# Fused attention, memory and expert kernel: scores of two heads as one step, padded memory tiles, one pace for attention

## The chip, the cores and the metric

The kernel runs on one core of one Trainium2 chip. The metric is the device time of one execution in microseconds (us). Before the change the median of three runs is 653.46 us (652.81 to 653.50).

## What is computed

The reference does two things in a row. The first is attention with a compressive memory, for 4 batches, 8 heads, 576 tokens and a head width of 64:

```
scores = q @ k.T / 8, causal
local  = softmax(scores) @ v
q_p    = elu(q) + 1
mem    = (q_p @ M_prev) / (q_p @ z_prev + 1e-6)
x      = g * mem + (1 - g) * local          # g = sigmoid(beta), one number per head
```

The second is a gated expert over all 2304 tokens, where `x` now has 512 columns (8 heads of 64):

```
out = (sigmoid(x @ w_gate) * (x @ w_val)) @ w_out      # 512 -> 1536 -> 512
```

Every product must keep single precision. The kernel gets there in two ways: as a plain fp32 matmul, which TensorE records as two instructions, or as three cheaper fp32r products of a high part and a remainder (high by high, high by low, low by high).

## The kernel before

**Groups.** The 2304 tokens are cut into six groups of 384 rows. Group 0 and group 5 hold the last 192 rows of two batches each ("tail" groups); groups 1 to 4 hold the first 384 rows of one batch each. Per group there is an attention part with four pairs of heads, and an expert part (`moe`) with 12 blocks of 128 hidden columns. The expert part of a group needs the attention results `xh`, `xl` of that group (high part and remainder, transposed).

**Attention of a pair.** The two heads of a pair lie on partitions 0 to 63 and 64 to 127 of a tile `kp`, so that the score matmul of one head uses the upper half of TensorE's rows and that of the other head the lower half. `scores` runs three times for a pair, one for each block of 128 queries. Up to the ninth pair (`n < SPLIT`) the scores are plain fp32 matmuls from `kp`; from then on they are fp32r products from split keys `kq`. Each head has a PSUM bank of its own. VectorE (DVE) adds the mask and finds the row's extreme in one pass (L505), ScalarE (ACT) takes the exponential (L514), `turn` transposes the result (on TensorE for pairs 0 to 7 and the last, by DMA in between), `values` multiplies by `v`, and `across` transposes the pair's `x` and writes `xh` on ACT and `xl` on DVE. `memory` multiplies the feature map `ph` by the tile `mb`, which holds `M_prev` and `z_prev` of two heads in block-diagonal form. GpSimd fills `mb` with zeros once (L298), and two DMAs of 66 KB write the two blocks.

**Expert.** For each block `f`: 24 matmuls of 384 columns (gate and value), then a tanh, a product, a copy and a subtraction that alternate between ACT and DVE, and nine matmuls of 512 columns of the block before (`down`). In group 0 the weights come as float64 and are converted on ACT and DVE first (`convert`: three tiles per block, four DVE instructions of 512 columns for each: L665, L667, L670 and a subtraction at L251); the result goes to DRAM, and groups 1 to 5 load it from there.

**What sets the order.** Nothing is issued while the Python loops run. Each instruction is recorded as a step with an engine, an estimated cost, the keys that it reads and writes, and a place in line (`Program.add`). `Program.issue` then plays all steps through a list schedule: whenever an engine is free, it takes the ready step that is first in line. The order of the instructions on each engine is what this yields, and the engines follow it strictly. Steps of TensorE in attention are moved up in line by 150 places (`LEAD`), and the estimated cost of TensorE is doubled up to `COLD`. The place in line comes from the main loop: while the expert part of group g is recorded, the ten steps per pair of group g + 1 are recorded between its pieces, spread by `SPREAD`.

Of the kernel before, what the change touches and what calls it, by code (L numbers as in the profile page):

```python
# [8 lines left out]
F32 = mybir.dt.float32  # L9
# [11 lines left out]
SPLIT = 9  # L21
# [4 lines left out]

SPREAD = 0.94


WHEN = (20, 36)  # L30

COLD = 12.0

# [11 lines left out]
class Program:  # L45
# [58 lines left out]
    def issue(self):  # L104
# [7 lines left out]
        engines = sorted({o[0] for o in ops})  # L112
        free = dict.fromkeys(engines, 0.0)
        link = 0.0
# [5 lines left out]
        for _ in ops:  # L120
# [16 lines left out]
            if e == "pe" and at < COLD:  # L137
                cost *= 2
            free[e] = at + cost
# [14 lines left out]
def tile_attention_memory_moe(  # L154
# [9 lines left out]
    nc = tc.nc  # L164
# [131 lines left out]

    def zeros(t, k):
        pool(520, lambda: nc.gpsimd.memset(t.rearrange("p b c -> p (b c)"), 0.0), [],  # L298
             [k + (j,) for j in range(2)], fast=True)

    def half(t, k):
# [14 lines left out]
    xl_r = Ring("xl", [128, KD, GT], F32R, 2)  # L316
    mb_r = Ring("mb", [128, HP, 2 * MC], F32, 2, init=zeros)
    ph_r = Ring("ph", [128, GT], F32, 2)
# [46 lines left out]
    def load_unit(g):  # L365
        mem[g] = []
        for b in batches(g):
            m, mk = mb_r.take()
            for j in range(2):
                r = slice(64 * j, 64 * j + 64)  # L370
                load(m[r, :, MC * j:MC * j + MC], mz[b, r].rearrange("p (a c) -> p a c", a=HP), 66, [], [mk + (j,)])
            mem[g].append((m, [mk + (j,) for j in range(2)]))

# [76 lines left out]
    def split(n):  # L450
# [8 lines left out]
        for e, (kp, kk) in enumerate(u.kp):  # L459
            for j in range(2):  # L460
# [8 lines left out]
                u.kq[j].append((kq, [kh, kd, kl], q, [kx, ql[j][1] + ("z",)]))  # L469

    def scores(n, c):

# [7 lines left out]
        def part(i, k0, k1):  # L480
# [8 lines left out]
            with pg.block():  # L489
                for e, q, m0, m1 in es * (n < SPLIT):  # L490
                    kp, kk = u.kp[e]
                    for j, r in enumerate(js):
                        pe(2 * m / 2385.0 + (0.07 if pair else 0.21), lambda kp=kp, j=j, r=r, q=q, m0=m0, m1=m1: nc.tensor.matmul(  # L493
                            out=sp[j][0][m0:m1, :m], lhsT=kp[r, u.qa + q:u.qa + q + m1 - m0],
                            rhs=kp[r, u.ka + k0:u.ka + k1], start=True, stop=True), [kk], [sp[j][1]])
                for e, q, m1 in ([(1, 64, 128), (0, 128, 64)] if pair else [(es[0][0], q0, 128)]) * (n >= SPLIT):
                    for j in range(2):
                        kq, kk, ql, kx = u.kq[j][e]
                        keys = kq[:, u.ka + k0:u.ka + k1]
                        out, out_k = sp[j][0][:m1, :m], sp[j][1]  # L500
                        matmul(out, kq[:, u.qa + q:u.qa + q + m1], keys, m, kk, [out_k], True, False)
                        matmul(out, ql[:, q:q + m1], keys, m, kk + kx, [out_k], False, True)
# [287 lines left out]

    def count(g):

        return HP * 10

    constants()
# [11 lines left out]
    att_banks[:] = [5, 6, 7]  # L807
    ready = 0
    for g in range(NG):
        while ready < g:  # L810
            y = step()
            if y:
                ready = y[1]
        done = 0
        steps = count(g) if g + 1 < NG else 0
        for i, _ in enumerate(moe(g)):
            while done * (7 * NF + 1) * SPREAD < (i + 1) * steps and ready == g:
                done += 1
                y = step()
# [10 lines left out]
def _layout(q, k, v, M_prev, z_prev, beta, moe_w_gate, moe_w_val, moe_w_out):  # L830
# [9 lines left out]
    mz = np.concatenate([M_prev, z_prev[..., None]], axis=3)  # L840
    mz = mz.reshape(B, H // 2, 2, D, D + 1).transpose(0, 2, 3, 1, 4)

    def up(x):
# [5 lines left out]
        "vp": vz,  # L849
        "mz": mz.reshape(B, 2 * D, (H // 2) * (D + 1)),  # L850
        "beta": beta,
# [25 lines left out]
```

## Time and profile before

| | |
|---|---|
| median of the runs | 653.46 us |
| the profiled execution | 652.48 us |
| its span, first to last instruction | 650.7 us |
| TensorE (PE) busy | 637.8 us, 98% |
| weight load (PEld) busy | 560.0 us, 86% |
| VectorE (DVE) busy | 422.0 us, 65% |
| ScalarE (ACT) busy | 303.5 us, 47% |
| GpSimd (POOL) busy | 8.6 us, 1% |
| DMA | 136.34 MB, mean 210 GB/s |

"Busy" is the time in which an engine has at least one instruction in flight. Matmuls overlap, so the mean duration of one (342 ns for 384 columns) is longer than the step from one to the next. The share of busy time is a mean over the whole span; the stages differ. Up to about 59 us only attention runs, from 59 us to about 172 us attention and the first expert part with the conversion of weights, then attention and expert parts without conversion, and from 574 us the last expert part alone.

### The profile page before, as it was taken

The numbers are of one execution on the slowest core, as the hardware profiler recorded it, in microseconds if no ns is written. First come the engines' busy times: TensorE is split into PE (matmuls) and PEld (weight loads), VectorE is DVE, ScalarE is ACT, GpSimd is POOL, SyncE is SP. The second block draws the span as 40 slices with busy tenths as digits, with TensorE's granted clock in tenths as the row PEclk, the third lists the DMA queues.
The fourth block names the chain that finished last, engine by engine and source line by source line (L and its number), as shares of the span: only waits on it lengthen the run. The fifth ranks groups of instructions, "written<-read, shape, count | busy, mean of one in ns | idle before, by whom it ended". The sixth has DMA issues, their size and how long they took to land.

```text
span 650.7 us, 12265 instructions
## 1 busy us (share of the span) xinstructions
PE 637.8 (98%) x4776; PEld 560.0 (86%) x4776; DVE 422.0 (65%) x1142; ACT 303.5 (47%) x590; POOL 8.6 (1%) x52
## 2 busy tenths in 40 slices
PE   6999999999999999999999999999999999999996
PEld 3656887878899999999999999989898899999995
DVE  3899989899837667656775656766757684411112
ACT  5878675667634424524543633433625242421111
POOL 3000000000000000000000000000000000000000
PEclk9999999999999999999999999999999999999999
DMA  8457878787996777779768879868879765264452
GB/s 291 159 195 225 285 261 304 233 320 240 245 295 197 180 201 209 218 207 223 202 178 214 219 204 201 210 177 249 252 181 219 174 183 157 74 235 145 179 171 72
DMA packets 90121, 136.34 MB, mean 210 GB/s; under 512 B 65744, under 2 KB 67792, under 8 KB 80848
## 3 DMA queue, kind: packets, MB, share of 16 engines
q1 hardware_dynamic: 90064, 135.57, 72.2%
q8 instruction: 37, 0.61, 0.4%
q14 instruction: 20, 0.16, 0.1%
HBM read 104.09 MB, written 17.30 MB: 187 GB/s over the span
## 4 chain that ended last, share of the span: by engine, by line
PE 92%; DVE 4%; DMA 2%; issue 1%; POOL 0%; ACT 0%; SPq 0%; POOLq 0%; DVEq 0%; ACTq 0%
PE bank L228 73%; PE bank L232 10%; PE bank L493 5%; PE bank L235 4%; DMA tl_wr<-pl_wr 1%; DMA mb<-in_mz_dram 1%; DVE a L505 1%; DVE kq_wt L251 0%; DVE ql L251 0%; DVE wt L667 0%; DVE wt L670 0%; DVE at L536 0%; DVE xm L251 0%; DVE xs L251 0%; DVE gl L251 0%
## 5 line engine op out<-in xcount | busy, mean ns | idle before, releaser
L228 PE MATMUL bank<-xh,wg 128*128 128x384 f32 x576 | 166.2, 342 | 0.2
L228 PE MATMUL bank<-xh,sv 128*128 128x384 f32 x576 | 165.5, 341 | 0.0
L228 PE MATMUL bank<-sv,gh 128*128 128x512 f32 x432 | 141.9, 399 | 0.0
L751 DVE SCALAR_TENSOR_TENSOR th<-th,bank 128x384 f32<-128x384 f32 x72 | 39.7, 551 | 116.4 <-PE bank L228 111.8
L228 PEld LDWEIGHTS bank<-xh,wg 128*128 128x128 f32 x576 | 105.0, 188 | 7.8 <-issue 3.0
L228 PEld LDWEIGHTS bank<-xh,sv 128*128 128x128 f32 x576 | 105.1, 188 | 1.4 <-issue 0.7
L514 ACT ACTIVATE a<-a,st 128x512 f32<-128x512 f32 (+4 forms) x144 | 81.5, 583 | 35.9 <-DVE st L505 35.3
L228 PE MATMUL bank<-xl,wg 128*128 128x384 f32 x288 | 97.7, 339 | 0.0
L228 PE MATMUL bank<-xl,sv 128*128 128x384 f32 x288 | 97.4, 338 | 0.0
L228 PEld LDWEIGHTS bank<-sv,gh 128*128 128x128 f32 x432 | 79.2, 188 | 12.5 <-issue 1.2
L749 ACT ACTIVATE th<-bank 128x384 f32<-128x384 f32 x72 | 35.2, 489 | 117.1 <-PE bank L228 116.7
L228 PE MATMUL bank<-sv,gl 128*128 128x512 f32 x216 | 85.9, 398 | 0.0
L241 ACT CAST gh<-th 128x384 fp32r<-128x384 f32 x72 | 36.8, 511 | 94.8 <-DVE th L751 94.3
L505 DVE CUSTOM_DVE_ANT_0 a<-bank,mask 128x128 f32<-128x128 f32 (+4 forms) x144 | 68.3, 485 | 19.0 <-PE bank L493 10.2
L228 PEld LDWEIGHTS bank<-xl,wg 128*128 128x128 f32 x288 | 54.1, 188 | 3.3 <-issue 0.5
L536 DVE COPY at<-tl_wr 128x256 uint16<-128x256 uint16 (+3 forms) x90 | 46.5, 519 | 15.5 <-DMA tl_wr<-pl_wr 15.3
L228 PEld LDWEIGHTS bank<-xl,sv 128*128 128x128 f32 x288 | 54.1, 188 | 0.6 <-issue 0.3
L251 DVE TENSOR_TENSOR gl<-th,gh 128x384 fp32r<-128x384 f32 x72 | 40.0, 555 | 20.4 <-ACT gh L241 19.9
L241 ACT CAST kq_wt<-kp 64x768 fp32r<-64x768 f32 (+2 forms) x60 | 38.0, 637 | 21.4 <-PE bank L228 20.5
L228 PEld LDWEIGHTS bank<-sv,gl 128*128 128x128 f32 x216 | 40.6, 188 | 8.3 <-issue 0.5
L493 PE MATMUL bank<-kp 64*128 64x512 f32 (+5 forms) x156 | 38.9, 523 | 4.0 <-DMA kp<-in_qk_dram 4.0
L530 DVE COPY pl_wr<-a 128x256 uint16<-128x256 uint16 (+3 forms) x90 | 41.7, 468 | 0.2
(72 smaller groups left out, 729.2 us busy)
## 6 DMA issues: line engine op xcount, KB each, us to landing
sv<-w SPq DMA_DIRECT2D x60, 1024.0 KB, 5.4
wr<-in_w_dram SPq DMA_DIRECT2D x36, 512.0 KB, 4.4
kp<-in_qk_dram SPq DMA_DIRECT2D x32, 384.0 KB, 3.8
w<-sv SPq DMA_DIRECT2D x12, 1024.0 KB, 6.4
out_dram<-ob SPq DMA_DIRECT2D x14, 256.0 KB, 5.0
vt<-in_vp_dram SPq DMA_DIRECT2D x8, 330.0 KB, 4.7
vr<-in_vp_dram SPq DMA_DIRECT2D x8, 330.0 KB, 5.4
vt<-in_vp_dram SPq DMA_DIRECT2D x8, 198.0 KB, 4.3
```

The costliest lines, as they stand in the source:

```text
L228: lambda: nc.tensor.matmul(out=out, lhsT=lhsT, rhs=rhs, start=start, stop=stop), r, w)
L232: lambda: nc.tensor.matmul(out=out, lhsT=lhsT, rhs=rhs, start=start, stop=stop), r, w)
L235: pe(0.110, lambda: nc.tensor.transpose(out=out, in_=in_, identity=identity), r, w)
L241: act(n, lambda: nc.scalar.copy(out=out, in_=in_), r, w)
L251: dve(n, lambda: nc.vector.tensor_tensor(out=out, in0=in0, in1=in1, op=op), r, w)
L493: pe(2 * m / 2385.0 + (0.07 if pair else 0.21), lambda kp=kp, j=j, r=r, q=q, m0=m0, m1=m1: nc.tensor.matmul(out=sp[j][0][m0:m1, :m], lhsT= ...
L505: dve(m + 60, lambda aj=aj, sj=sj, pj=pj: nc.vector.tensor_tensor_reduce(out=aj[:, k0:k1], in0=pj[:, :m], in1=mk, scale=-0.125, scalar=3.0 ...
L514: act(W + 120, lambda aj=aj, sj=sj: nc.scalar.activation(out=aj[:, :W], in_=aj[:, :W], func=AF.Exp, scale=-1.0, bias=sj[:, len(ns) - 1:len ...
L530: dve(2 * W, lambda src=src, pl=pl: nc.vector.tensor_copy(out=pl.rearrange("p (two w) -> p two w", two=2), in_=src), [ak], [pk], fast=True)
L536: dve(2 * W, lambda tl=tl, dst=dst: nc.vector.tensor_copy(out=dst, in_=tl.rearrange("p (two w) -> p two w", two=2)), [lk], [key], fast=True)
L749: act(GT, lambda: nc.scalar.activation(out=th, in_=pg_[:, :GT], func=AF.Tanh, scale=0.5), [pg_k], [th_k])
L751: dve(GT, lambda: nc.vector.scalar_tensor_tensor(out=th, in0=th, scalar=1.0, in1=pv[:, :GT], op0=ALU.add, op1=ALU.mult,), [th_k, pv_k], [t ...
```

## The change

The two heads' score matmuls of a piece become one step of the schedule, so nothing can be placed between them, and the step waits for both heads' banks. `mb` is laid out with its zeros by the host and comes in one DMA of 266 KB; the fill on GpSimd is gone. The steps of attention are no longer counted anew in each group: one count runs through all groups, ten steps per pair, with a lead of `AHEAD` = 8. The planner's constants are other ones: the higher cost of TensorE at the start is 1.5 times up to 8 us (2 times up to 12 us before), and all engines start at 0.7.

```diff
-SPREAD = 0.94
+AHEAD = 8
...
-COLD = 12.0
+COLD = 8.0
+
+START = 0.7
...
-        free = dict.fromkeys(engines, 0.0)
+        free = dict.fromkeys(engines, START)
...
             if e == "pe" and at < COLD:
-                cost *= 2
+                cost *= 1.5
...
-    mb_r = Ring("mb", [128, HP, 2 * MC], F32, 2, init=zeros)
+    mb_r = Ring("mb", [128, HP, 2 * MC], F32, 2)
...
             m, mk = mb_r.take()
-            for j in range(2):
-                r = slice(64 * j, 64 * j + 64)
-                load(m[r, :, MC * j:MC * j + MC], mz[b, r].rearrange("p (a c) -> p a c", a=HP), 66, [], [mk + (j,)])
-            mem[g].append((m, [mk + (j,) for j in range(2)]))
+            load(m.rearrange("p a c -> p (a c)"), mz[b], 266, [], [mk])
+            mem[g].append((m, [mk]))
...
+    def heads(u, es, sp, js, k0, k1):
+
+        for e, q, m0, m1 in es:
+            kp, _ = u.kp[e]
+            for j, r in enumerate(js):
+                nc.tensor.matmul(
+                    out=sp[j][0][m0:m1, :k1 - k0], lhsT=kp[r, u.qa + q:u.qa + q + m1 - m0],
+                    rhs=kp[r, u.ka + k0:u.ka + k1], start=True, stop=True)
...
-                for e, q, m0, m1 in es * (n < SPLIT):
-                    kp, kk = u.kp[e]
-                    for j, r in enumerate(js):
-                        pe(2 * m / 2385.0 + (0.07 if pair else 0.21), lambda kp=kp, j=j, r=r, q=q, m0=m0, m1=m1: nc.tensor.matmul(
-                            out=sp[j][0][m0:m1, :m], lhsT=kp[r, u.qa + q:u.qa + q + m1 - m0],
-                            rhs=kp[r, u.ka + k0:u.ka + k1], start=True, stop=True), [kk], [sp[j][1]])
+                if n < SPLIT:
+                    pe(4 * m / 2385.0 + 0.3, lambda: heads(u, es, sp, js, k0, k1),
+                       [u.kp[e][1] for e, *_ in es], [sp[j][1] for j in range(2)])
...
     att_banks[:] = [5, 6, 7]
-    ready = 0
+    ready, made = 0, 0
     for g in range(NG):
         while ready < g:
             y = step()
+            made += 1
             if y:
                 ready = y[1]
-        done = 0
-        steps = count(g) if g + 1 < NG else 0
         for i, _ in enumerate(moe(g)):
-            while done * (7 * NF + 1) * SPREAD < (i + 1) * steps and ready == g:
-                done += 1
+            while made < (g + (i + 1) / (7 * NF + 1)) * HP * 10 + AHEAD and ready + 1 < NG:
+                made += 1
                 y = step()
```

The order of all engines changes in places. Three places follow. The first is TensorE in the attention of group 0, some 30 us after the start. `kp0` and `kp1` hold the two batches of the third pair, `kp2` and `kp3` those of the second; a score row of 128x512 is one head. Before:

```order
L493 MATMUL bank7_70<-kp0_101 128x512
L493 MATMUL bank3_66<-kp2_103 64x256
L493 MATMUL bank3_66<-kp3_104 64x256
L235 MATMUL bank4_67<-idn_71,xs0_131 128x128 x3
L493 MATMUL bank0_63<-kp0_101 128x512
L232 MATMUL bank1_64<-mb0_105,ph0_107 128x130
L232 MATMUL bank1_64<-mb1_106,ph0_107 128x130 x2
L232 MATMUL bank1_64<-mb0_105,ph0_107 64x130
L493 MATMUL bank7_70<-kp1_102 128x512
L493 MATMUL bank4_67<-kp2_103 64x256
L493 MATMUL bank4_67<-kp3_104 64x256
```

And in the change:

```order
L472 MATMUL bank7_70<-kp0_101 128x512
L472 MATMUL bank0_63<-kp0_101 128x512
L237 MATMUL bank4_67<-idn_71,xs0_131 128x128 x3
L234 MATMUL bank1_64<-mb0_105,ph0_107 128x130
L234 MATMUL bank1_64<-mb1_106,ph0_107 128x130 x2
L234 MATMUL bank1_64<-mb0_105,ph0_107 64x130
L472 MATMUL bank7_70<-kp1_102 128x512
L472 MATMUL bank0_63<-kp1_102 128x512
L472 MATMUL bank3_66<-kp2_103 64x256
L472 MATMUL bank4_67<-kp2_103 64x256
L472 MATMUL bank3_66<-kp3_104 64x256
L472 MATMUL bank4_67<-kp3_104 64x256
```

Before, other work stood between the two heads of all three score pieces; in the change the heads stand side by side. Over the program there are 41 unbroken runs of score rows before and 26 in the change. The 15 that go are three of 512 columns, one of 320 and three of 256 columns in group 0, and four of 256, two of 384 and two of 128 columns in pairs 4 to 8.

The second place is the start of the queue of SyncE, which issues all DMAs. `vt` are values, `bt` is beta. Before:

```order
L259 DMA bt_74<-in_beta_dram 128x8
L259 DMA vt0_108<-in_vp_dram 128x660
L259 DMA mb0_105<-in_mz_dram 64x4x65
L259 DMA mb0_105<-in_mz_dram 64x4x65
L259 DMA mb1_106<-in_mz_dram 64x4x65
L259 DMA mb1_106<-in_mz_dram 64x4x65
L259 DMA vt1_109<-in_vp_dram 128x660
```

And in the change:

```order
L261 DMA bt_74<-in_beta_dram 128x8
L261 DMA mb0_105<-in_mz_dram 128x520
L261 DMA mb1_106<-in_mz_dram 128x520
L261 DMA vt0_108<-in_vp_dram 128x660
L261 DMA vt1_109<-in_vp_dram 128x660
```

Both memory tiles now stand ahead of the first values, as two DMAs in place of four.

The third place is VectorE near the end of the conversion of weights, up to the row that finishes the value weights of the last block (`sv2<-wt2`). `th` and `gl` belong to the gate of a block, `xs` and `xl` to a pair's result, `kq` to the split keys of a later pair. Before:

```order
L251 TENSOR_TENSOR xs1_143<-bank7_70,rs1_144 128x384
L665 TENSOR_SCALAR wt2_142<-wt2_142 128x512
L251 TENSOR_TENSOR xs1_143<-xs1_143,xm1_128 128x384
L667 SCALAR_TENSOR_TENSOR wt2_142<-wr1_139,wt2_142 128x512
L505 ISA a0_112,st2_120<-bank6_69,mask_72 128x256
L505 ISA st2_120 128x1
L670 SCALAR_TENSOR_TENSOR wt2_142<-wr1_139,wt2_142 128x512
L251 TENSOR_TENSOR xl1_155<-bank5_68,xh1_154 128x384
L665 TENSOR_SCALAR wt3_146<-wt3_146 128x512
L505 ISA a1_113,st3_121<-bank7_70,mask_72 128x256
L505 ISA st3_121 128x1
L251 TENSOR_TENSOR sv2_150<-wt2_142,sv2_150 128x512
```

And in the change:

```order
L253 TENSOR_TENSOR wg11_100<-wt1_140,wg11_100 128x512
L667 TENSOR_SCALAR wt2_142<-wt2_142 128x512
L507 ISA a3_119,st5_125<-bank6_69,mask_72 128x384
L507 ISA st5_125 128x1
L669 SCALAR_TENSOR_TENSOR wt2_142<-wr1_139,wt2_142 128x512
L753 SCALAR_TENSOR_TENSOR th0_149<-th0_149,bank4_67 128x384
L672 SCALAR_TENSOR_TENSOR wt2_142<-wr1_139,wt2_142 128x512
L253 TENSOR_TENSOR kq_wt0_161<-kp1_102,kq_wt0_161 64x384
L667 TENSOR_SCALAR wt3_146<-wt3_146 128x512
L253 TENSOR_TENSOR gl0_151<-th0_149,gh0_150 128x384
L253 TENSOR_TENSOR sv2_152<-wt2_142,sv2_152 128x512
```

The last pair's result of group 1 (`xl1`) is now finished before this stretch, and a gate, two score passes of 384 columns and split keys stand ahead of the last value weights. Counted from the program's start up to that row, the change has these on VectorE that stood behind it before: two score passes of 384 columns with their 128x1 reads, one `th`, one `gl`, one `kq` row of 384 columns and one copy of 256 columns.

## Rows read from the trace of the kernel before

**Rows 1.** The page, busy time: us, share of the span, instructions.

```profile
PE 637.8 (98%) x4776; PEld 560.0 (86%) x4776; DVE 422.0 (65%) x1142; ACT 303.5 (47%) x590; POOL 8.6 (1%) x52
```

**Rows 2.** The page, chain that ended last, by engine and share.

```profile
PE 92%; DVE 4%; DMA 2%; issue 1%; POOL 0%; ACT 0%; SPq 0%; POOLq 0%; DVEq 0%; ACTq 0%
```

**Rows 3.** Waits of PE: us in total, times, the longest.

```profile
PE bank L493 <- DMA kp<-in_qk_dram: 4.0, 1, 4.0
PE bank L232 <- DMA mb<-in_mz_dram: 2.0, 1, 2.0
PE bank L228 <- DVE st L505: 0.6, 2, 0.5
```

**Rows 4.** Stretches: busy us of PE, PEld, DVE, ACT, POOL; PEclk, DMA share, GB/s.

```profile
4.00:6.00 2.00, 2.00 (x6) 0.98 (x8) 0.00 (x0) 1.18 (x3) 1.23 (x6) 1.00 0.99 310
...
50.00:60.00 10.00, 9.46 (x150) 7.15 (x150) 9.93 (x31) 9.56 (x20) 0.00 (x0) 1.00 0.91 283
60.00:172.00 112.00, 112.00 (x841) 92.73 (x840) 103.30 (x264) 77.95 (x155) 1.06 (x8) 1.00 0.79 263
172.00:300.00 128.00, 127.70 (x901) 117.84 (x900) 82.24 (x241) 54.42 (x106) 0.69 (x5) 1.00 0.80 218
```

**Rows 5.** Chain in order of time, scores and transposes: start, us, what.

```profile
16.47 1.03 PE bank L235 x8
17.50 1.06 PE bank L493 x4
26.45 0.70 PE bank L493 x8
30.39 1.05 PE bank L493 x2
61.97 0.58 PE bank L493 x4
63.24 0.62 PE bank L493 x2
70.94 0.59 PE bank L235 x4
111.78 0.84 PE bank L493 x2
145.84 0.42 PE bank L493 x2
```

**Rows 6.** Chain in order of time, the start.

```profile
2.13 0.94 POOL mb L298 x2
4.35 6.00 DMA mb<-in_mz_dram
10.48 2.39 PE bank L232 x8
12.87 1.47 PE bank L235 x6
14.34 2.13 PE bank L493 x16
18.56 1.23 PE bank L232 x8
```

**Rows 7.** Waits of DVE, 20 to 172 us: total, times, the longest.

```profile
DVE a L505 <- PE bank L493: 2.7, 6, 0.7
...
DVE th L751 <- PE bank L228: 2.3, 3, 1.4
```

**Rows 8.** Timeline: VectorE's last value weights, TensorE's first use of them.

```profile
162.44 0.69 DVE L251 TENSOR_TENSOR sv<-wt,sv 128x512 fp32r<-128x512 f32 x1
...
163.65 0.28 DVE L530 COPY pl_wr<-a 128x256 uint16<-128x256 uint16 x1
...
169.37 0.39 PE L228 MATMUL bank<-xh,sv 128*128 128x384 f32 x1
```

**Rows 9.** Groups by line, DVE: a row of 384 columns; busy us, mean ns.

```profile
L251 DVE TENSOR_TENSOR xs<-bank,rs 128x384 f32<-128x384 f32 x24 | 13.3, 555 | 0.6
```

More of the change, by code (lines that the diff above doesn't have):

```diff
@@ L295, in gates @@
             out=ga, in0=gs, scalar1=-1.0, scalar2=1.0, op0=ALU.mult, op1=ALU.add), ["gs"], ["ga"])
-    def zeros(t, k):
-        pool(520, lambda: nc.gpsimd.memset(t.rearrange("p b c -> p (b c)"), 0.0), [],
-             [k + (j,) for j in range(2)], fast=True)
     def half(t, k):
@@ L789, in step @@
         return y
-    def count(g):
-        return HP * 10
     constants()
@@ L841, in _layout @@
     mz = mz.reshape(B, H // 2, 2, D, D + 1).transpose(0, 2, 3, 1, 4)
+    mb = np.zeros((B, 2, D, H // 2, 2, D + 1), mz.dtype)
+    for j in range(2):
+        mb[:, j, :, :, j] = mz[:, j]
     def up(x):
@@ L849, in _layout @@
         "vp": vz,
-        "mz": mz.reshape(B, 2 * D, (H // 2) * (D + 1)),
+        "mz": mb.reshape(B, 2 * D, H * (D + 1)),
         "beta": beta,
```

## Prediction

> **What bounds the kernel now.** I read the page's busy times first: TensorE has work in flight for 98% of the span, the next engine, VectorE, for 65% [rows 1]. Busy time alone proves little, so the chain of waits comes second: 92% of it is TensorE [rows 2]. Third, TensorE's own waits: 4.0 us for the first keys, 2.0 us for the memory tile at the start, 0.6 us later on VectorE, and nothing else above half a microsecond [rows 3]. So after about 10.5 us the kernel is as long as the row of instructions on TensorE, and what shortens that row shortens the kernel, unless another engine becomes late. The stretches show where one could: from 50 to 60 us VectorE is busy for 9.93 of 10 us, and from 60 to 172 us for 103.30 of 112 us; after 172 us it has slack, 82.24 of 128 us [rows 4]. Until 172 us the kernel has two full engines, afterwards one.
>
> **Scores of two heads side by side.** The chain shows what an interruption costs. Four records (two heads of 512 columns) side by side take 1.06 us; two records, one head alone, take 1.05 us [rows 5]. The second head is free if it follows the first at once, since the two use different halves of the array's rows, and costs a full 1.05 us if anything stands between. In the order before there are 15 such interruptions, in the change none. The pieces cost, alone: 1.05 us for 512 columns, 0.58 us for a 256-column piece of the tail groups (two batches, four records), 0.62 us for 128x256, 0.84 us for 128x384, 0.42 us for 128x128; a 320-column piece with both heads takes 0.70 us and I take the same for its half [rows 5]. The sum is 3 x 1.05 + 3 x 0.58 + 0.70 + 4 x 0.62 + 2 x 0.84 + 2 x 0.42 = 10.6 us. Each interruption also cuts a run of other work in two. Four transposes between scores take 0.59 us, eight take 1.03 us [rows 5]: 0.11 us each and 0.15 us for the run itself. A cut between other kinds may cost less, so I take 0.10 us: 15 x 0.10 = 1.5 us. TensorE's row gets 12.1 us shorter, between 10.6 (cuts for nothing) and 12.9 (0.15 us each). All 15 lie before 172 us.
>
> A step now waits for both banks. Behind it on TensorE stands the rest of the program. Before, the first head could start while the second bank was still being read, but then stood alone for the full price; the wait costs at most the time of one score pass on VectorE, 0.55 us for 384 columns [rows 9], and only where VectorE is late, which is priced below.
>
> **The start.** The first product with the memory tile starts at 10.48 us, when its DMA lands, and TensorE had idled for 2.0 us [rows 3, 6]. The fill on GpSimd goes, but it ended at 3.07 us and the DMA that mattered began at 4.35 us [rows 6], so that alone is worth nothing. What counts is the queue: ahead of and with the first tile stood four key tiles of 393 KB, 330 KB of values and 132 KB of memory (2.03 MB by the sizes in the load calls); now it is four key tiles and 266 KB, 1.84 MB. At 310 GB/s [rows 4] the tile comes 0.6 us earlier. Its former pieces of 260 bytes per row become rows of 2080 bytes, the first tile alone is now enough for the first product, and transposes fill in while the second lands, so up to the whole 2.0 us can go. The first values land later, behind 532 KB of memory tiles (1.7 us at that rate), and nothing waits for them: their first product comes after the second pair's memory products, which start at 18.56 us [rows 6].
>
> There is a second term. After the idle time TensorE works at half pace: the eight memory products from 10.48 us take 2.39 us, the same eight at 18.56 us take 1.23 us; six transposes take 1.47 us against about 0.8 us; sixteen score records (320 and 256 columns) 2.13 us against 0.70 + 0.58 [rows 5, 6]. That is 1.16 + 0.67 + 0.85 = 2.7 us lost, although the granted clock in the rows stands at 1.00, the level of 2.4 GHz [rows 4]; the durations fit 1.2 GHz. The Trainium skill, "TensorE: Matmul & The Clock Gate", Part 1, says that the array's clock is throttled by default and that activity releases it. By that rule a start without idle time would reach full pace sooner and give back up to these 2.7 us; the trace agrees that work after idle time is slow, and cannot show when the pace would rise without it. Bounds of the start: 0.6 us gained (the tile alone) to 4.7 us (idle time and slow pace both gone). I take 3.2 us: most of the idle time, 1.7, and about half of the slow pace, 1.5.
>
> **What VectorE gives back.** The place is the first expert part. VectorE finishes the value weights of block 11 at 163.1 us, TensorE uses them at 169.4 us: 6.2 us of margin [rows 8]. TensorE's row before that use is 12.1 us shorter. VectorE's row before it gets longer by the instructions that the new pace puts ahead: five of 384 columns at 0.555 us [rows 9], a copy of 0.28 us [rows 8] and two short reads, 3.2 us. A common shift of both engines by the earlier start cancels. So VectorE would be late by 12.1 + 3.2 - 6.2 = 9.1 us if it kept all its idle time. From 20 to 172 us it waited 2.7 + 2.3 = 5.0 us for TensorE [rows 7]; these waits go when TensorE is ahead. Its waits for ScalarE stay. TensorE waits for 9.1 - 5.0 = 4.1 us; bounds 0 (VectorE also loses its other waits and the order hides the rest) and 9.1 us. After 172 us VectorE has slack, and nothing is lost or regained by it.
>
> The Trainium skill, "TensorEngine Tiling (Array Packing)", section PSUM Bottleneck, speaks against the change here: tiling speeds up TensorE but not the emptying of PSUM, which may become the bottleneck. The trace bears it out by half, VectorE's 103.30 of 112 us [rows 4]. Followed to its end it is the first rival below.
>
> **Pace and lead.** In the later groups the orders differ by little, and the work is the same. The values and the result of a group's last pair now come inside the first block of the next expert part in more places, so the margin at each handover is thinner; before, TensorE's waits on VectorE there came to 0.6 us in all [rows 3]. I add 1.0 us, bounds 0 and what the slower rival says. The DMAs of the memory tiles grow by 1.06 MB, 3.4 us of transfer at 310 GB/s spread over six groups, and each tile is asked for in the pair before its use: nothing.
>
> **Sum.** -12.1 - 3.2 + 4.1 + 1.0 = -10.2 us. The profiled execution took 652.48 us (span 650.7 and 1.8 around it) and would take 642.3. The median of the runs shown is 653.46, 1.0 above it; on that base I forecast 643.3 us, on its own between 640 and 647.
>
> **Rivals.**
> First, VectorE sets the pace until 172 us: no wait of its own is recovered, and the start gives the smallest gain. -12.1 - 0.6 + 9.1 + 1.0 = -2.6: 650.9 us. For it: 9.93 of 10 us busy from 50 to 60 us [rows 4], and the longer row ahead of the last weights. Against it: over half of its waits were for TensorE itself [rows 7].
> Second, all of it arrives: the start gains 4.7 us, VectorE is not late, handovers cost nothing. -16.8: 636.7 us. For it: VectorE's total idle time until 172 us, 8.7 us from 60 us on alone [rows 4], nearly covers the 9.1. Against it: waits for ScalarE are in that.
> Third, slower: the handovers become the wait. At each of the five, the chain from the last pair's values to its `xl` must be over before TensorE can finish the first block's sums: on VectorE two rows of the result and the remainder at 0.555 us [rows 9], three short rows, transposes and a copy on ScalarE, some 3 us. Fully exposed five times on top of a late VectorE: -12.1 - 0.6 + 9.1 + 15 = +11.4: 664.9 us. It decides the sign from 0.7 us per handover on. For it: the thinner place of the values. Against it: other matmuls still stand between, and the same pattern cost 0.6 us in all before.
> Fourth, no change: the first rival with a handover of 0.7 us five times: 653.4 us.
>
> **Chances.** The forecast 0.50, first rival 0.20, second 0.16, fourth 0.06, third 0.08. A difference of 0.2%, 1.3 us, is about what a measurement tells from none. Forecast, first and second are faster: 0.86; same 0.06; slower 0.08. The range 638 to 650.5 leaves out about half of the second rival, the fourth, the third and the outer edge of the first, 0.2.
>
> **What would show it.** Right: all score runs have four or eight records, TensorE's score time in chain pieces falls by about 10 us; the first memory product starts before 10 us; small waits of TensorE on VectorE, or on ScalarE behind it, appear between about 100 and 165 us, some 4 us in all; the last expert part is as long as before. Wrong: waits of TensorE of more than 9 us up to 172 us (first rival), none at all (second), or several microseconds at the start of each expert part (third); or the first memory product no earlier than 10.48 us, which would take back the term of the start.

## The result and the profile after

The changed kernel takes 646.66 us (median of 4 runs, 645.55 to 647.76) against 653.34 us (4 runs of the kernel before, 652.81 to 653.50): ratio 0.9899, 95% interval 0.9887 to 0.9910, 6.7 us less. The forecast was 643.3 us, its range 638 to 650.5. The profiled execution took 646.17 us, its span is 644.4 us, 6.3 less than before.

The page, busy time and chain by engine, against [rows 1, 2]:

```profile
PE 625.7 (97%) x4776; PEld 554.8 (86%) x4776; DVE 421.1 (65%) x1142; ACT 300.6 (47%) x590; POOL 7.8 (1%) x50
PE 86%; DVE 7%; ACT 4%; DMA 2%; issue 1%; SPq 0%; ACTq 0%
```

TensorE's busy time fell by 12.1 us (637.8 before), the span only by 6.3. The other 5.8 us are idle time: span less busy is 18.7 us, 12.9 before. VectorE and ScalarE together hold 11% of the chain, 4% before. TensorE's waits say for whom, against [rows 3] (engine, line, releaser: us in total, times, longest):

```profile
PE bank L472 <- DMA kp<-in_qk_dram: 3.8, 1, 3.8
PE bank L237 <- DVE xm L253: 1.8, 2, 1.0
PE bank L237 <- DVE xs L253: 1.5, 2, 1.1
PE bank L234 <- DVE st L507: 1.3, 2, 0.8
PE bank L237 <- ACT a L516: 1.2, 2, 0.8
PE bank L234 <- DMA mb<-in_mz_dram: 1.1, 1, 1.1
PE bank L230 <- ACT th L751: 0.9, 2, 0.6
```

The wait for the memory tile is 1.1 us, it was 2.0. The waits on L237 and L234 for VectorE and ScalarE are new: transposes and memory products in attention. The stretches say where. First a row of the kernel before that was not shown, busy us of PE, PEld, DVE, ACT, POOL, then PEclk, DMA share, GB/s:

```profile
20.00:60.00 40.00, 39.29 (x489) 25.49 (x488) 37.33 (x112) 34.61 (x68) 0.47 (x4) 1.00 0.62 197
```

And the changed kernel, against this row and [rows 4]:

```profile
20.00:60.00 40.00, 34.67 (x477) 24.69 (x473) 35.80 (x108) 32.17 (x64) 0.69 (x6) 1.00 0.59 190
60.00:172.00 112.00, 110.57 (x863) 94.96 (x862) 105.95 (x272) 79.20 (x159) 0.66 (x6) 1.00 0.84 292
172.00:300.00 128.00, 126.44 (x888) 116.15 (x887) 81.18 (x234) 52.85 (x103) 0.64 (x5) 1.00 0.75 210
```

TensorE is idle for 5.33 us of the 40 between 20 and 60 us (0.71 before), for 1.43 in the first expert part (0.00), for 1.56 from 172 to 300 us (0.30). After 300 us there is nothing to tell. Most of what did not arrive was lost in the attention of group 0.

The start, in the chain in order of time (start, us, what), against [rows 6]:

```profile
3.07 6.99 DMA mb<-in_mz_dram
...
10.19 0.46 PE bank L234 x2
10.65 0.66 PE bank L237 x6
11.31 0.81 PE bank L234 x6
...
19.50 0.50 PE bank L234 x12
```

The DMA lands at 10.06 us, hardly earlier, so the first memory product starts at 10.19 us against 10.48. But TensorE is at full pace there: the eight memory products (two and six, 0.46 and 0.81 us) take 1.27 us in all, they took 2.39 us, and six transposes take 0.66 us, they took 1.47 us. The first values product starts at 19.50 us; in the kernel before the chain has it as

```profile
22.57 3.18 PE bank L232 x104
```

so 3.1 us were gained here, with the same score records and five more transposes done before it. Twenty microseconds later the chain looks like this, where before it was almost all TensorE until 48 us:

```profile
39.02 0.57 DVE wt L669
39.66 0.40 DVE a L507
40.07 0.47 DVE xs L253
...
41.42 0.60 DVE a L507
...
42.72 0.47 DVE xl L253
...
43.28 0.57 DVE wt L672
43.92 0.60 DVE wt L669
44.52 0.47 DVE xm L253
44.99 0.39 DVE a L507
45.42 2.06 ACT a L516 x3
47.48 1.23 ACT at L243 x3
```

From 39.02 to 48.71 us the chain does not touch TensorE. It is VectorE's own row: score passes (a), results (xs, xm, xl), and between them the conversion of weights (wt), then ScalarE's exponentials and copies. TensorE has no other work then: the expert part starts at 56 us. The scores wait for no bank: of all of TensorE's waits in this trace, the only one at a score matmul is that for the first keys.

The place that the prediction named, against [rows 8]: VectorE's last value weights and TensorE's first use of them, and VectorE's waits for TensorE from 20 to 172 us, against [rows 7]:

```profile
158.56 0.68 DVE L253 TENSOR_TENSOR sv<-wt,sv 128x512 fp32r<-128x512 f32 x1
...
160.88 0.34 PE L230 MATMUL bank<-xh,sv 128*128 128x384 f32 x1
```

```profile
DVE a L507 <- PE bank L472: 0.6, 1, 0.6
...
DVE th L753 <- PE bank L230: 0.2, 1, 0.2
```

The margin shrank from 6.2 to 1.6 us and was not used up. Of the 1.43 us of idle time from 60 to 172 us, 1.0 us stands before 64 us, at the transposes of group 0's fourth pair, and 0.41 us right behind this place, where TensorE waits for split keys that VectorE makes in the same stretch:

```profile
163.99 0.30 PE L230 MATMUL bank<-kq_wr 128*128 128x128 f32 x1 [0.41 <-DVE kq_wr L253]
```

VectorE's waits for TensorE fell from 5.0 to 0.8 us.

### The profile page after: what moved, and what is told of

The parts are those of the page before. It is cut to its first block, busy times and chain, and to the rows that moved or that the text cites. A ratio compares the mean times of both kernels' runs of the same rounds, so it can differ in the third digit from the quotient of the medians.

```text
span 644.4 us, 12258 instructions
## 1 busy us (share of the span) xinstructions
PE 625.7 (97%) x4776; PEld 554.8 (86%) x4776; DVE 421.1 (65%) x1142; ACT 300.6 (47%) x590; POOL 7.8 (1%) x50
## 4 chain that ended last, share of the span: by engine, by line
PE 86%; DVE 7%; ACT 4%; DMA 2%; issue 1%; SPq 0%; ACTq 0%
PE bank L230 71%; PE bank L234 9%; PE bank L237 3%; PE bank L472 2%; DVE a L507 1%; DMA tl_wr<-pl_wr 1%; DMA mb<-in_mz_dram 1%; ACT a L516 1%; ACT at L243 1%; DVE wt L669 1%; DVE xs L253 1%; DVE wt L672 0%; ACT th L751 0%; DVE wt L667 0%; DVE xl L253 0%
## 5 line engine op out<-in xcount | busy, mean ns | idle before, releaser
L230 PEld LDWEIGHTS bank<-sv,gh 128*128 128x128 f32 x432 | 79.6, 188 | 12.1 <-issue 0.3
L516 ACT ACTIVATE a<-a,st 128x128 f32<-128x128 f32 (+4 forms) x144 | 80.3, 582 | 19.9 <-DVE st L507 19.2
L237 PEld LDWEIGHTS bank<-idn,a 128*128 128x128 f32 x184 | 20.6, 140 | 12.9 <-issue 2.9
```

Source lines behind the costliest of these rows:

```text
L230: lambda: nc.tensor.matmul(out=out, lhsT=lhsT, rhs=rhs, start=start, stop=stop), r, w)
L237: pe(0.110, lambda: nc.tensor.transpose(out=out, in_=in_, identity=identity), r, w)
L516: act(W + 120, lambda aj=aj, sj=sj: nc.scalar.activation(out=aj[:, :W], in_=aj[:, :W], func=AF.Exp, scale=-1.0, bias=sj[:, len(ns) - 1:len ...
```

## The experiments

Eight kernels give every combination of three parts of the change: H, the scores as one step; S, what concerns the start (padded memory tiles and the planner's constants); P, the one pace with its lead. Four came after the result of the first ones. In the expectations of the first four, three theories say where TensorE's new waits come from. T1: VectorE has too much to do up to 172 us. T2: a step of scores needs two free banks at once, and the chain between the engines is long. T3: the new pace puts attention ahead of the conversion on VectorE. In the run without conversion T1 and T2 return, for group 0 alone: T1 is that the conversion stands in the way, T2 that the chain itself is too long. T4 came later: what TensorE saves is kept only as far as group 2's attention comes earlier too, whose tiles (`kq`, `pl`, `tl`) lie in the conversion's buffers.

**Scores alone (H), on the kernel before.**

```diff
-                for e, q, m0, m1 in es * (n < SPLIT):
...
+                if n < SPLIT:
+                    pe(4 * m / 2385.0 + 0.3, lambda: heads(u, es, sp, js, k0, k1),
+                       [u.kp[e][1] for e, *_ in es], [sp[j][1] for j in range(2)])
```

> The kernel before with the two heads' scores as one step, and nothing else of the change. Theory 1: TensorE's row is 12.1 us shorter, and what the whole change lost again (about 5 to 6 us) went into waits of TensorE for VectorE, which has too much to do up to 172 us; without the start's gain of 3.1 us this gives 646 to 649 us, with new waits of TensorE of 4 to 6 us between 20 and 172 us. Theory 2: the waits come from the pairing itself, since one step needs two free banks: the same time, 646 to 649 us. Theory 3: the waits come from the new pace, which puts attention ahead of the conversion on VectorE: with the old pace they are absent, 641 to 643 us.

652.76 us, ratio 0.9995 (0.9986 to 1.0005): no change. All three theories missed. TensorE's busy time fell by 7.5 us, to 630.3; its idle time rose by 7.7, to 20.6. The windows between 264 and 280 us and the chain show the new loss, the handover to group 2:

```profile
264.00:266.00 2.00, 1.62 (x39) 1.24 (x37) 1.41 (x5) 0.99 (x2) 0.00 (x0) 1.00 1.15 338
266.00:268.00 2.00, 0.57 (x12) 0.43 (x12) 1.38 (x6) 0.60 (x1) 0.00 (x0) 1.00 0.98 410
268.00:270.00 2.00, 1.30 (x6) 0.80 (x6) 1.91 (x5) 1.42 (x3) 0.00 (x0) 0.81 1.11 343
270.00:276.00 6.00, 5.75 (x19) 5.58 (x19) 5.27 (x17) 4.32 (x9) 0.17 (x1) 0.50 0.45 107
```

```profile
268.02 0.56 DVE xs L251
...
269.05 0.56 DVE ql L251
269.63 0.57 DVE xm L251
270.25 7.83 PE bank L228 x29
```

TensorE is ahead, waits for the result of group 2's last pair behind other rows of VectorE, and after these 2.5 us of idle time in 6 us the granted clock stands at 0.50, the level of 1.2 GHz, for 6.8 us (269.2 to 276 us in the clock's records). TensorE is busy for 6.0 of them, which costs half of that, 3.0 us. Without this, busy time would have fallen by 10.5 us: this is what the 15 interruptions cost here, 12.1 predicted.

**The pace alone (P), on the kernel before.** The diff is the last part of the change's.

> The kernel before with the one count of steps and the lead of eight, and nothing else. Theories 1 and 2: the row of TensorE is not shorter and its waits not longer, 652 to 655 us. Theory 3: the new pace alone makes TensorE wait for VectorE, 657 to 660 us.

657.96 us, ratio 1.0061 (1.0045 to 1.0078): slower, in the range of T3. The start was 2 us later, and the last weights were converted at 174.3 us instead of 166.3. Interruptions are not the reason: the trace has the same 41 runs of score rows as before. TensorE waits longer for the memory tile (3.2 us at once, 2.04 before) and then works at a granted clock of 0.50 from 12.0 to 18.8 us; and at 156 us it waits 2.0 us for the row `xs` of VectorE.

**The changed kernel with less work on VectorE, and the kernel before with as much less.** In both the 36 instructions of L672 (L670 before) are left out, 0.685 us each: the low bits of the float64 weights are not merged in.

```diff
-        dve(DM, lambda: nc.vector.scalar_tensor_tensor(
-            out=t, in0=lo, scalar=29, in1=t, op0=ALU.logical_shift_right, op1=ALU.bitwise_or,
-        ), [wr_k, t_k], [t_k])
+        dve(DM, lambda: None, [wr_k, t_k], [t_k])
```

> The changed kernel, whose conversion leaves out the lowest three bits of each weight's mantissa: 36 VectorE instructions of 0.685 us are not issued, but stay in the plan, so every other instruction keeps its place in the order. VectorE has 24.6 us less to do up to 172 us. Theory 1: TensorE's waits for VectorE shrink by 4 to 6 us, 640.5 to 643 us. Theory 2: the waits stay, since they come from two banks and from the chain between engines: 645.5 to 647.5 us.

> The kernel before with the same 36 VectorE instructions left out of the conversion (the lowest three bits of each weight's mantissa), order otherwise unchanged. Theories 1 and 2: TensorE's row decides and had no waits for VectorE, 652 to 653.7 us. If VectorE decided before as well: 650 us or less.

644.31 us, ratio to the kernel before 0.9869 (0.9847 to 0.9891), 2.4 us less than the changed kernel; and 653.21 us, ratio 0.9998 (0.9988 to 1.0009), for the kernel before. The kernel before is where T1 and T2 had it; the changed kernel falls between T1's range and T2's. So VectorE did not bound the kernel before at all, and seems to bound the changed one a little: 24.7 us off VectorE's row are worth 2.4 us. The two intervals just touch and one of the four executions took 647.28 us, but TensorE's idle time agrees, 16.7 us against 18.7 with the same busy time. TensorE's idle time from 20 to 60 us is 4.84 us, hardly less than 5.33: of the instructions left out two lie on the chain before 56 us (28.50 and 43.28 us).

**The other four combinations.** S, HS, HP and PS, on the kernel before, with the parts of the change's diff.

> The kernel before with the padded memory tiles and the planner's new constants alone; scores and pace as before. In all runs so far the time from the first block of group 2's expert part to the end is 367 to 368 us, so the question is what comes earlier up to there. Theory T4 (what comes earlier on TensorE is kept only as far as group 2's attention also comes earlier, which is tied to the end of the conversion by its buffers): the start is 3 us earlier, the conversion too, so all of it is kept: about 650 us. Rival A (the start's gain is eaten by the group-0 attention as the scores' gain was): 653 us. Rival B (the start gives nothing without the new pace): 653 us and the first values product still at 22 to 23 us.

> The whole change but the pace. T4: TensorE arrives early at group 2's attention and waits for it as with the scores alone, because the old count records the pairs 8 to 11 late; only what the start gives to the conversion is kept: 649 to 651 us, with TensorE's waits for VectorE of 3 us or more between 255 and 275 us. Rival A (the pace plays no part, the scores gain as soon as the start is better): 646 to 647 us as the changed kernel. Rival B (start and scores compete in the attention of group 0, nothing is gained): 653 us.

> Scores as one step and the one pace, without padded memory tiles and new constants. T4: the pace brings group 2's attention forward by its lead, so that the scores' gain is no longer waited away at that handover; the start is not earlier, so 3 us less gain than the whole change, 649 to 650 us (up to 652 if the start is as slow as in the run of the pace alone, whose first values product came at 24.4 us). Rival A (the pace only does harm, as it did alone: 4.6 us slower): 657 us. Rival B (the start plays no part): 646 to 647 us.

> The whole change but the scores. T4: the pace alone was 658 us, with the slow start and a conversion that ended 8 us later; the start gives 3 to 5 us back, the conversion stays late because TensorE's row in the attention of group 0 is full: 652 to 655 us. Rival A (the pace was slower only through its bad start): 647 to 650 us, and the scores give the rest. Rival B (the pace delays the conversion by what it records ahead, whatever the start): 656 to 658 us.

All eight (median; TensorE's busy and idle time, and the idle time in three stretches, of the profiled execution):

| parts | us | ratio (95%) | busy | idle | 20 to 60 | 60 to 172 | 172 to 300 |
|---|---|---|---|---|---|---|---|
| none (first job) | 653.34 | 1 | 637.8 | 12.9 | 0.71 | 0.00 | 0.30 |
| S | 655.46 | 1.0027 (1.0013 to 1.0042) | 643.6 | 16.1 | 1.35 | 2.26 | 1.94 |
| P | 657.96 | 1.0061 (1.0045 to 1.0078) | 639.5 | 17.8 | 0.72 | 2.12 | 0.75 |
| PS | 657.00 | 1.0053 (1.0038 to 1.0068) | 638.8 | 16.4 | 2.98 | 0.62 | 2.16 |
| H | 652.76 | 0.9995 (0.9986 to 1.0005) | 630.3 | 20.6 | 4.08 | 0.91 | 3.33 |
| HP | 652.87 | 0.9990 (0.9973 to 1.0007) | 631.6 | 21.5 | 4.42 | 2.53 | 1.98 |
| HS | 649.29 | 0.9944 (0.9924 to 0.9964) | 629.0 | 20.7 | 4.72 | 1.60 | 2.80 |
| HPS | 646.66 | 0.9899 (0.9887 to 0.9910) | 625.7 | 18.7 | 5.33 | 1.43 | 1.56 |

Of the expectations, that of HS held (649 to 651 us by T4); S was to be 650 by T4 and came slower than before, which no theory had; HP came 0.9 us above T4's upper end (652), PS 2 us above T4's, where its rival B had it. Compare each kernel with H to the one without: it has at least 7.5 us less busy time and 2.4 to 3.7 us more idle time from 20 to 60 us. The parts do not add up: S and P each make the kernel slower alone, and H gains 0.6 us alone, 6.2 with S, 5.1 with P, 10.3 with both. One reason is in the order of the instructions: with P and S and without H, 17 pairs of scores are interrupted, 12.9 us at the prediction's prices, against 15 and 10.6 us before. With H that goes. It is a small part: P alone has the runs of before, and 2.3 us are not the difference between 0.6 and 10.3. The rest stays open. S's own profile was its slowest execution (661.42 us; its 11 runs span 653.84 to 661.42), with this row:

```profile
30.00:40.00 10.00, 10.00 (x23) 3.94 (x22) 5.04 (x16) 4.13 (x7) 0.12 (x1) 0.51 0.14 41
```

The table's 643.6 us of busy time hold 13.7 us at half clock; P's hold 6.5, HP's 6.6, H's 6.0 and HS's 9.4, those of the other three none in the clock's records. With half of that taken out, H shortens busy time by 10.5 us (none to H), 12.4 (S to HS), 8.0 (P to HP) and 13.1 (PS to HPS). S's longer time is mostly the clock too: its two executions with a mean clock of 1.000 took 653.84 and 654.40 us, level with the kernel before.

**Group 0's attention without conversion beside it.** The changed kernel; the weights of blocks 0 and 1 are loaded only when the third pair's result is there.

```diff
-WHEN = (20, 36)
+WHEN = (37, 42)
...
-        load(wr, wi[f, :, i * DM:(i + 1) * DM], 524, [], [wr_k])
+        load(wr, wi[f, :, i * DM:(i + 1) * DM], 524, [pairs[2].x_k] if f < 2 else [], [wr_k])
```

> The changed kernel, but the loads of the weights of blocks 0 and 1 wait until the third pair's result is there (and are recorded at steps 37 and 42 of group 0 instead of 20 and 36), so that VectorE and ScalarE have no conversion work while group 0's first three pairs run. In the changed kernel TensorE is idle for 5.3 us from 20 to 60 us. Theory T1 (the conversion stands in the way of the attention's chain on VectorE): the idle time from 20 us to about 48 us falls from some 4 us to 1 us or less, the third pair's values come 3 us earlier; then TensorE waits for the weights, and the kernel is slower in all, 655 to 665 us. Theory T2 (the chain itself, score to reduction to exponential to transposes to values, is longer than TensorE's remaining work, whatever else VectorE does): the idle time until about 48 us stays within 1 us of what it is, and the total is as slow.

657.67 us, ratio 1.0076 (1.0043 to 1.0109), as slow as both theories had it. The windows from 20 to 48 us of this kernel:

```profile
20.00:30.00 10.00, 10.00 (x156) 7.29 (x157) 6.10 (x24) 7.18 (x15) 0.23 (x2) 1.00 0.27 87
30.00:40.00 10.00, 9.21 (x150) 6.39 (x146) 5.03 (x19) 6.96 (x14) 0.00 (x0) 1.00 0.36 111
40.00:48.00 8.00, 7.21 (x67) 4.67 (x66) 5.14 (x19) 5.94 (x11) 0.23 (x2) 1.00 0.63 211
```

And of the changed kernel:

```profile
20.00:30.00 10.00, 8.70 (x135) 5.64 (x131) 8.03 (x26) 8.21 (x17) 0.23 (x2) 1.00 0.39 122
30.00:40.00 10.00, 8.68 (x142) 6.37 (x142) 9.19 (x28) 8.58 (x17) 0.00 (x0) 1.00 0.82 259
40.00:48.00 8.00, 6.50 (x41) 3.93 (x41) 8.00 (x26) 6.05 (x11) 0.23 (x2) 1.00 0.74 259
```

TensorE's idle time there falls from 4.12 to 1.58 us. Between 40 and 48 us VectorE was busy without a gap (8.00 of 8.00), and now is for 5.14. So T1 holds for about 2.5 of the 4.1 us and T2 for the rest. The start of this run was 2 us later, so the split is rough. Counted from the first pair's values to the third's, T1's share is larger: 25.7 us here (21.69 to 47.41), 29.2 in the changed kernel (19.43 to 48.59), 30.9 before (22.50 to 53.35), so 3.4 us go with the conversion. The run with the left-out instructions had seemed to speak against T1; it took away only two pieces of this chain, this run takes all the conversion steps of VectorE and ScalarE out of it, eleven before 48 us. It moves the loads of these weights as well, but in the changed kernel no engine except GpSimd waits for a DMA from 20 to 48 us.

**No lead.** The changed kernel with `AHEAD = 0`.

> The changed kernel with a lead of 0 instead of 8 steps. Measure: the time from VectorE's product of the last block of group 1 to that of the first block of group 2, 10.3 us in the kernel before, 13.7 in the changed kernel, 17.7 with the old count and the rest of the change. T4 (the lead brings group 2's attention forward and so spares the wait at that handover): this time is 17 us or more, with a stretch at half clock, and the total is 649 to 652 us. Rival A (the lead costs as much in the first expert part as it gives at the handover): 646 to 647 us. Rival B (the lead only does harm): 643 to 645 us.

646.80 us, ratio 0.9907 (0.9885 to 0.9929): the same as the changed kernel, as rival A had it. The time between the two blocks is 14.4 us, not 17. T4 was wrong on the lead. What differs between HS (649.29 us; its profiled execution took 651.49, the longest of five) and these two is the stretch from 264 to 268 us: HS has

```profile
264.00:268.00 4.00, 1.90 (x35) 1.53 (x30) 2.94 (x8) 0.60 (x1) 0.00 (x0) 0.88 1.03 402
268.00:272.00 4.00, 3.30 (x12) 2.71 (x11) 3.87 (x12) 2.90 (x5) 0.13 (x1) 0.50 0.45 138
```

and the kernel without lead

```profile
264.00:268.00 4.00, 2.62 (x15) 2.42 (x15) 3.77 (x9) 3.14 (x7) 0.11 (x1) 1.00 0.85 235
268.00:272.00 4.00, 4.00 (x24) 4.00 (x24) 3.35 (x12) 2.99 (x7) 0.00 (x0) 1.00 0.47 124
```

In HS 2.1 us of these four are idle, and behind them stands the half clock; without the lead it is 1.4 us, and the clock stays at 1.00. Two of HS's five executions had a mean clock of 0.997 and took 648.50 and 649.29 us, still more than any of the changed kernel's, so the clock is not all of it. Why the old count, which also starts anew in each group, brings group 2's last result 4.4 us later than the new one with no lead (270.1 against 265.7 us) though the conversion ends at the same time (163.2 and 162.6 us) stays open.

**Part of the conversion on GpSimd.** A try at a faster version: the remainders of blocks 2 to 11, for the output weights alone, and for all three.

```diff
-        sub(nc.vector, lo_out, tf, hi_out.bitcast(F32), DM, [t_k, kh], [kl])
+        sub(nc.gpsimd if f >= 2 and i == 2 else nc.vector, lo_out, tf, hi_out.bitcast(F32), DM, [t_k, kh], [kl])
```

> The changed kernel with ten of the conversion's 36 remainders (the output weights of blocks 2 to 11) on GpSimd instead of VectorE: a try at a faster version. It takes 10 x 0.55 = 5.5 us off VectorE before 165 us. T4 (the end of the conversion sets group 2's attention, its handover and so the end; leaving out 36 instructions of 0.685 us, 24.7 us, gave 2.4 us): 0.5 us by proportion, 645 to 646.5 us. Rival A (GpSimd is slow and these weights come too late for their block): 648 us or more. Rival B (GpSimd's work slows VectorE's instructions down): no gain, VectorE's 512-column instructions longer than 0.685 us beside it.

> The same with all three remainders of blocks 2 to 11 on GpSimd, 30 x 0.55 = 16.5 us off VectorE. T4: by proportion to the run with 24.7 us left out, 1.6 us: 644.5 to 645.5 us. Rival A (the gate's remainders come too late from GpSimd, TensorE waits for weights): 650 us or more. Rival B (GpSimd slows VectorE down): 646 to 649 us, with longer VectorE instructions.

652.88 us, ratio 0.9996 (0.9984 to 1.0008), and 665.86 us, ratio 1.0208 (1.0177 to 1.0239): 6 and 19 us slower than the changed kernel. T4's numbers missed by far. Groups by line and form of the first of the two (busy us, mean ns), then L672 again and the group on GpSimd (duration min/median/max):

```profile
L672 DVE SCALAR_TENSOR_TENSOR wt<-wr,wt 128x512 int32<-128x512 int32 x36 | 25.8, 718 | 0.3
L253 DVE TENSOR_TENSOR sv<-wt,sv 128x512 fp32r<-128x512 f32 x14 | 12.5, 891 | 1.2 <-ACT sv L243 1.2
...
L672 DVE SCALAR_TENSOR_TENSOR wt<-wr,wt x36: 645/684/1312, 20.2 to 163.6; 128x512 int32<-128x512 int32 x36
...
L255 POOL TENSOR_TENSOR sv<-wt,sv x10: 1282/1566/1859, 63.1 to 165.4; 128x512 fp32r<-128x512 f32 x10
```

And of the changed kernel:

```profile
L672 DVE SCALAR_TENSOR_TENSOR wt<-wr,wt 128x512 int32<-128x512 int32 x36 | 24.5, 684 | 0.2
L253 DVE TENSOR_TENSOR sv<-wt,sv 128x512 fp32r<-128x512 f32 x24 | 16.0, 685 | 1.6 <-ACT sv L243 1.6
```

GpSimd takes 1.57 us for what takes VectorE 0.68, and VectorE's own instructions get longer beside it: the mean of the remainders that stayed is 891 ns instead of 685. It is few of them that do: the median of L672 stays at 684 ns. Nine VectorE instructions, each begun while a subtraction ran on GpSimd, took 0.6 to 1.1 us more than the median of their kind, 8.1 us in all; the ten subtractions had taken 6.9 us off VectorE. VectorE is busy for 107.4 us from 60 to 172 us, 1.5 more than without the help. Rival B held, in the second kernel A with it. No run beat the changed kernel with all its work.

## Why the prediction was right, and where it was not

The time fell within the range, and the sign and the mechanism were right: TensorE's row is shorter, and a part is given back in waits for VectorE and ScalarE. Point by point:

| step | predicted | measured |
|---|---|---|
| scores side by side | -12.1 | -10.5, busy time of H against none, the half clock taken out |
| start | -3.2 | -3.1, first values product |
| VectorE gives back | +4.1, at block 11 | +6.0: 4.6 from 20 to 60 us, 1.4 from 60 to 172 us |
| handovers | +1.0 | +1.3, idle time from 172 to 300 us |
| sum | -10.2 | -6.3; -6.7 between the medians, -6.3 between the profiled executions |

That the sum meets the measured gain so well is partly chance: the terms come from different profiles, and the first is 8.0 to 13.1 us by which pair of kernels it is taken from. There is luck in the time too: the prediction adds its terms up, but its largest is worth 0.6 us alone, and 10.3 only beside the other two parts.

**Scores.** The single term that carries the forecast stands, 1.6 us too large. The 10.6 us for the interruptions alone fit what was measured, and the changed kernel agrees: its busy time is 12.1 us less, of which 1.9 us are pace at the start. The 0.10 us for each cut run of other work was not separately tested. From P to HP, with the same score runs, only 8.0 us came; why stays open.

**Start.** The size is right, its split is not. The DMA lands 0.3 us earlier (0.6 predicted), and the first memory product missed the sign set for it, before 10 us; 1.1 us of idle time went in the first 20 us (1.7 predicted), and the rest is pace. The profile after has its first clock record at 8.6 us, that of before at 16.5 us, and the eight memory products take 1.27 instead of 2.39 us. So the 1.00 that the prediction read in the row of 4 to 6 us [rows 4] is no record of the clock, and its durations told the pace rightly. S alone, however, gained nothing in the end.

**What VectorE gives back: the step that failed.** The prediction looked for the wait where TensorE's row meets VectorE's last value weights, at block 11. The margin there did shrink, and VectorE got 4.2 of its 5.0 us of waits back, but 1.6 us of margin are left, and TensorE is idle for only 1.43 us from 60 to 172 us, 1.0 of it for group 0's last pair; what is late there is one row of split keys, by 0.41 us. The waits stand in group 0's attention, mostly before any expert work, at 26 to 64 us where 100 to 165 was predicted, and are larger. There TensorE has only the attention itself to do: each score pair that gets shorter brings the next transposes sooner, and these need VectorE's and ScalarE's results. The run without conversion shows that 2.5 to 3.4 us of it are conversion steps between the attention's own. The trace of the kernel before showed it: 37.33 us of VectorE's busy time in the 40 from 20 to 60 us, and 9.93 of 10 at its end [rows 4]. The prediction read that row as a sign for the whole stretch until 172 us, summed margins over it, and priced the seven or so interruptions of group 0 as kept.

**Pace.** It was priced at 1.0 us by its handovers alone. The combinations show that it costs 4.6 us alone, changes nothing beside H (652.76 and 652.87) and gives 2.6 us beside both (HS to HPS), and its lead is worth nothing: 646.80 without it. The forecast did not see that the parts depend on each other.

**Rivals.** The first (650.9 us) had the right kind of bound, but VectorE's amount of work is worth 2.4 us when 24.7 us of it go. The second is excluded by the idle time. The third, exposed handovers, happened in the kernels H and HS at one handover out of five, with a half clock behind it, and hardly in the changed kernel.

## What to carry to other kernels

A margin summed over a long stretch hides the place where an engine has nothing else to do: look for each piece of saved time at what the engine does next, and whether that is ready. A part of a change that is worth 10 us beside the others can be worth nothing alone, so test parts both alone and taken away from the whole. An engine that looks idle is no free helper if its work makes the busy one's instructions longer.

## What the runs showed of the hardware

A short wait of TensorE can cost more than itself. In H, 2.5 us of idle time between 264 and 270 us were followed by 6.8 us at a granted clock of 0.50, 3.0 us of loss; in HS 2.1 us of idle time in four did the same. In the changed kernel 5.33 us of idle time, in pieces of up to 1.06 us over 40 us, left the clock at 1.00. At the start a wait for the memory tile of 1.15 us (changed kernel) or 1.24 us (no lead) left it there as well; behind 1.61 us (HS) stand 3.4 us at 0.50, behind 3.2 us (P) 6.8 us. In S the clock fell to 0.51 from 30 to 40 us although TensorE was busy for 9.27 of the 10 us before; what it answered to there stays open. The mean granted clock of an execution accounts for S's spread: 1.000 with 653.84 us, 0.993 with 657.13 and 657.46, 0.989 with 661.42; 0.011 of 650 us are 7.2 us, the difference is 7.6. It does not do so for the kernel before, where 0.993 stands with 652.80 us and 1.000 with 653.91: there, in the profile shown, the half pace ahead of the first clock record counts as 1.00.

GpSimd's 512-column subtraction lengthens a VectorE instruction that begins beside it: the longest L672 is 1312 ns with ten such subtractions and 1685 ns with thirty, against 694 ns without. The Trainium skill, "GPSIMD Engine Reference", section 1, Specifications, says that the two engines share their interfaces to SBUF and that VectorE's instructions with two SBUF inputs, or in a 2-port mode, contend. The trace agrees for two inputs, as eight of the nine long instructions have; the ninth, an L667 with one input, took 1427 ns against 418, and in which mode it runs no row shows.
